# A fused attention and expert kernel: five expert units from a table built beside the scatters, and turned remainders by transposes

## The chip, the cores and the metric

The kernel runs on one core of a Trainium2 chip. The time is the device time of one execution in microseconds (us). Five engines of the core work side by side, each through its own instructions in order: PE (TensorE, the matrix engine), ACT (ScalarE), DVE (VectorE), POOL (GpSimd) and SP (SyncE, which issues most DMAs). PSUM is the memory that PE writes its results to, in banks of 2 KB a partition; SBUF is the memory that the engines compute from. An engine's instruction waits at the head of its queue until the semaphores it needs are up.

## The reference

An attention with a threshold, and behind it a mixture of experts in which each token goes to one expert:

```
q, k, v: [8, 8, 576, 64]; x: 4608 tokens of 512; 8 experts, w1 [8, 512, 1024], w2 [8, 1024, 512]
scores = q @ k.T / 8
scores = where(scores >= max(scores) - tau, scores, -1e9)
x = (softmax(scores) @ v), heads side by side         # tokens of 512
e = argmax(x @ w_gate);  gate = softmax(x @ w_gate)[e];  eom = sigmoid(x @ w_output_gate)
out[token] = gate * eom[e] * (relu(x @ w1[e]) @ w2[e])
```

## The kernel before

**Attention.** The first half of the program runs over 32 units, each one head of two batches (the two halves of the partitions). A period m takes two units in nine steps, s = 0 to 8: four tiles of 128 queries of the one, a tile with the last 64 queries of both, four tiles of the other. There are sixteen periods. In a step PE computes the scores of tile g (L137, into PSUM tiles `ps`), DVE copies them with the row maximum (L148), POOL makes the threshold (L155), ACT takes the exponentials (L162) and DVE masks and sums (L175). Two steps later the tile of probabilities `p` is turned, keys onto partitions: eight blocks of 64 columns by 16 transposes (L217, `pt`, copied out by ACT at L220 or L225), and the remainder, the last 128 columns, by `remainder`. In between PE issues matmuls of `av_units` (L239), a generator that multiplies the turned probabilities `PTa` (256 queries) or `PTb` (320 queries) with the values into one bank `pa`: ten matmuls to a half, of which a step takes 4, 6 or 8, so that a half stays open from one step to the next; the copy at L244 ends it.

The remainder comes in two forms. In a step that also issues the rows of x (s = 1 and 5; L330 copies them out of the banks `pr` and `pa`), two transposes of 128x64 are put in unused columns of these banks (L201) and ACT copies them from there (L202). In every other step two matmuls with the identity as the moving side (L206, 64x128, PE in another row and column mode than its neighbours) write `pr`, and ACT copies that (L209).

**Routing.** A `Router` holds a queue of generators that are advanced a step at a time between other work: they find each token's expert (`route`), place it by a running count (`place`, `init_units`, `finish`), and scatter its row to a DRAM buffer `xs` with POOL DMAs (L473). `finish` writes zero rows behind each expert's last token (the pads, again L473), then computes on DVE, in operations on 1x8 to 1x352 elements, which expert and which row each later unit has.

**Experts.** A unit is a run of rows of one expert. It has eight steps f; in a step `first(f)` does twelve matmuls (L945 to L947: three for each of four chunks, since each operand is split in a high and a low part), ACT makes `hh` by relu (L949) and DVE the rest `hl` (L950). `second` of the step before it does three matmuls of 512 columns for each tile of 128 rows (L966 to L968). Steps 5 and 6 turn the next unit's rows (`prep`, L931), and each weight chunk (four to a unit, 1 MB) is split by ACT (L761) and DVE (L764). The next unit's rows are gathered by one DMA that SP issues (L908). Units 0 and 1 are the first 384 rows of experts 0 and 1 (the early units, gathered from tokens that are already scattered); then six units of 512 with static experts, four `Pair` units of 256 rows whose expert is read from a table, and one `Flex` of 128 rows interleaved with unit 10: 4992 rows in all, 52 weight chunks, where there are 4608 tokens. `rest` is a loop for what is left over. The transition is the part from unit 0 to the start of unit 2: the last routing, the token scatters, the pads and the table happen there.

Of the kernel before, what the change touches and what calls it, by code (L numbers as in the profile page):

```python
# [8 lines left out]
F32 = mybir.dt.float32  # L9
# [11 lines left out]
class Attention:  # L21
# [12 lines left out]
    def __init__(self, ctx, tc, ident, qkv, tau, wg, shape, router):  # L34
# [45 lines left out]
        self.loaded, self.sums, self.rinv, self.lt, self.sumup = {}, {}, {}, {}, None  # L80
# [116 lines left out]
    def remainder(self, dst, p, pair=None):  # L197
# [12 lines left out]

    def blocks(self, dst, p, late=False):
        nc, id_, hs, RB = self.nc, self.ident, self.half, self.NK - 1
        pt = self.ps_t.tile([P, 1024], F32, name="pt")
        for b in range(RB):
            for h in range(2):
                o, k0 = h * 512 + b * 64, (b + b // 4) * P
                nc.tensor.transpose(pt[:, o : o + 64], p[hs[h], k0 : k0 + P], id_[hs[h], hs[h]])  # L217
        if len(dst) == 1:
# [8 lines left out]
    def av_units(self, u):  # L227
# [4 lines left out]
        for half in range(2):  # L232
            PT, q0 = (self.PTb, self.QA) if half else (self.PTa, 0)
            N = PT.shape[2]
            pa = self.ps_a.tile([P, 512], F32, name="pa")
            for i in range(self.NB + 1):
# [6 lines left out]
                if i == self.NB:  # L243
                    nc.scalar.copy(X[:, q0 : q0 + N], pa[:, 0:N])  # L244
                yield
# [57 lines left out]

    def run(self, hooks):
# [4 lines left out]
        for g in range(G + self.TAIL):  # L309
# [55 lines left out]
            if lu is not None and lu in xls:  # L365
                self.logits(lu, xls.pop(lu))
                if lu == self.nu - 1:
                    self.logit_sums(0)
                    self.logit_sums(1)
# [8 lines left out]
class Router:  # L378
    NPAIR = 4

    def __init__(self, ctx, tc, ntok, E, DM, early, esize, cut):
# [12 lines left out]
        self.A = E * self.CAP + 2 * P  # L394
# [9 lines left out]
        self.ecap = c.tile([P, E], F32, name="ecap")  # L404
        self.asc = c.tile([P, E], F32, name="asc")
# [3 lines left out]
        for e in range(E):  # L409
            nc.gpsimd.memset(self.ebase[:, e : e + 1], float(e * self.CAP + self.base[e]))  # L410
            nc.gpsimd.memset(self.elim[:, e : e + 1], float(e * self.CAP + esize) if e < early else -1.0)
# [19 lines left out]
        self.prows = c.tile([1, 2, self.NPAIR], I32, name="pairs")  # L431
        self.total = c.tile([1, 1], I32, name="total")
        self.odd = ctx.enter_context(tc.tile_pool(name="rodd", bufs=1))
        self.ripe = False
        self.xrows, self.queue, self.pending, self.placed, self.tables = {}, [], None, None, []
        self.gate, self.kind = None, None

# [11 lines left out]
    def init_units(self):  # L449
        E = self.E  # L450
        parts = [(self.xs[self.A :, :], "itok")]
        for e in range(self.early, E + 1):
            n = self.base[e] if e < E else 2 * P
            parts.append((self.xs[e * self.CAP : e * self.CAP + n, :], "itok"))
        for dst, group in parts:
            for r in range(0, dst.shape[0], P):
# [4 lines left out]
                yield None  # L461
# [23 lines left out]
    def route(self, bp, rows, LX):  # L485
# [77 lines left out]
        G.tensor_copy(rows[:, :, self.DM], sc)  # L563
        yield False
# [30 lines left out]
    def finish(self, ctx):  # L595
        nc, E = self.nc, self.E
        sm = ctx.enter_context(self.tc.tile_pool(name="rfin", bufs=1, reuse_waits="tile"))
        V = nc.vector
        pad = sm.tile([P, E], F32, name="padf")
        padi = sm.tile([P, E], I32, name="padi")  # L600
        V.tensor_scalar(pad, self.cnt, self.pid, None, op0=ALU.add)
        V.tensor_copy(padi, pad)
# [6 lines left out]
        row = lambda n, name, dt=F32: sm.tile([1, n], dt, name=name)  # L609
        ni, nj, nf, np, m0, v = row(E, "ni", I32), row(E, "nj", I32), row(E, "nf"), row(E, "np"), row(E, "m0"), row(E, "v")  # L610
        cp, ci, cm = row(E + 1, "cp"), row(E + 1, "ci"), row(E + 1, "cm")
        V.tensor_tensor(nf, self.cnt[0:1], self.ebase[0:1], op=ALU.subtract)
        V.tensor_scalar(nf, nf, float(P - 1), None, op0=ALU.add)
        V.tensor_copy(ni, nf)
        yield False
        V.tensor_scalar(ni, ni, 7, None, op0=ALU.arith_shift_right)
        V.tensor_scalar(ni, ni, 0, None, op0=ALU.max)
        V.tensor_scalar(nj, ni, 1, None, op0=ALU.arith_shift_right)
        V.tensor_copy(nf, ni)
        V.tensor_copy(np, nj)  # L620
        yield from self.sums(cp, np)
        yield from self.table(sm, "p", self.prows, cp, 2 * P, self.ebase[0:1])
        self.tables.append("p")
        yield False
        V.tensor_scalar(cm, cp, float(self.NPAIR), None, op0=ALU.min)
        V.tensor_tensor(m0, cm[:, 1:], cm[:, 0:E], op=ALU.subtract)
        V.scalar_tensor_tensor(nf, m0, -2.0, nf, op0=ALU.mult, op1=ALU.add)
        V.scalar_tensor_tensor(v, m0, float(2 * P), self.ebase[0:1], op0=ALU.mult, op1=ALU.add)
# [45 lines left out]
class Experts:  # L674
    RB, NW, YB = 4, 4, 4
    PAIRS = (2, 4, 6, 8)
    FLEX = 10
# [18 lines left out]
    def open(self):  # L696
# [7 lines left out]
        for name, bufs in (("y", 4), ("x", 2), ("h", 2)):  # L704
# [39 lines left out]
    def emit_out(self, y, keys, n):  # L744
        nc, DM = self.nc, self.rt.DM
        yo = self.yp.tile([P, DM], F32, name="yo")
        sc = keys[0][:, n : n + 1]
        if n % 2:
            nc.scalar.activation(yo, y, AF.Copy, scale=sc)
        else:  # L750
# [3 lines left out]
            out_offset=bass.IndirectOffsetOnAxis(ap=keys[1][:, n : n + 1], axis=0),  # L754
# [15 lines left out]
    def first_chunk(self):  # L770
        w, (a, b) = self.split_w(self.raws.pop(0))
        self.ready.append(w)
        self.done = 2
# [3 lines left out]
    def begin(self, nstatic):  # L777
        rt = self.rt
        make = [lambda e=e: Base(self, e) for e in range(rt.E)]
        for s, at in enumerate(self.PAIRS):  # L780
            make.insert(rt.early + at, lambda s=s: Pair(self, s))
        self.make, self.units, self.flex = make, {}, None
        self.seq = []
        for i in range(len(make)):
            for g in range(4):
                self.seq.append((i, g))
                if i == self.FLEX:
                    self.seq.append((None, g))
        self.nload = self.done = self.used = 0
        self.halves, self.ready = [], []  # L790
        for _ in range(self.RB):
            self.load_next()

    def unit(self, i):
        if i is None:
            if self.flex is None:
                self.flex = Flex(self, 0)
            return self.flex
# [4 lines left out]
    def load_next(self):  # L803
        if self.nload < len(self.seq):
            i, g = self.seq[self.nload]
            self.nload += 1
            self.raws.append(self.load(self.unit(i).e, g, self.rt.gate if self.nload <= self.RB else None))

    def split_until(self, n):
        while self.done < min(n, 2 * len(self.seq)):  # L810
# [6 lines left out]
            if not self.halves:  # L817
                self.load_next()
# [5 lines left out]
    def run(self):  # L824
        rt, nun = self.rt, len(self.make)
        self.split_until(4)
        prev, fin = None, False
        for i in range(nun):
            b, final = self.unit(i), i == nun - 1
            late = 4 if i == rt.early - 1 else 0  # L830
            for f in range(8):
# [3 lines left out]
                if i == self.FLEX + 1 and f == 1:  # L835
                    self.flex.second(turned)
                    self.flex.finish()
# [11 lines left out]
                if i == self.FLEX and f % 2:  # L849
                    self.flex.step(f // 2, self.take())  # L850
                if i == self.FLEX + 1 and f == 0:
                    turned = self.flex.transposed()
# [3 lines left out]
                self.split_until(2 * self.used + (4 if f % 2 else 3))  # L856
# [4 lines left out]
                if i == self.FLEX - 1 and f == 7:  # L861
                    self.flex.gather()
                if i == self.FLEX and f == 0:
                    self.flex.prep()
# [4 lines left out]
                for _ in range(4):  # L869
                    rt.advance(True)  # L870
                if not rt.queue and not fin:
# [294 lines left out]
```

## Time and profile before

| | before |
|---|---|
| time, median of 3 (lowest, highest) | 968.69 us (967.88, 969.49) |
| the profiled execution: time, span | 967.93 us, 966.2 us |
| PE busy | 948.4 us (98%) |
| DVE, ACT, POOL busy | 690.3 us (71%), 592.3 us (61%), 339.0 us (35%) |
| granted TensorE clock, mean | 0.995 |
| instructions | 22101 |

A row of a timeline gives the start, the duration, the engine, the line, the operation with its output and inputs by the program's names, its size and a count of equal instructions that follow each other; behind it in brackets the idle time of the engine ahead of it and what ended it. The duration of a matmul covers its way through the array, so that matmuls that follow each other overlap; their price is the distance of two starts. The 1.7 us between the span and the profiled time lie outside the trace.

### The profile page before, as it was taken

The page shows a single profiled execution, that of the slowest core. Times are in us where ns is not written, and L with a number is a line of the kernel's source. Part 1 is how long each engine was busy: PE and PEld are TensorE (multiplying, and loading weights), DVE is VectorE, ACT ScalarE, POOL GpSimd, SP SyncE. Part 2 cuts the span into 40 slices and gives each one's busy share as a digit, 9 for nine tenths or more (in the row PEclk, how much of TensorE's full clock was granted, in tenths as well). Part 3 has the DMA queues.
Part 4 walks back from the last instruction along what each step waited for, and adds up shares of the span by engine and source line. Part 5 has one row for each costly group of instructions (what it writes and reads, how often), then busy time and mean ns, then how long its engine had stood idle before and what let it go on. Part 6 is the DMA issues. An engine that isn't in the chain of part 4 may idle for free. (4 is left out here: it accounts for less than half of the span.)

```text
span 966.2 us, 22101 instructions
## 1 busy us (share of the span) xinstructions
PE 948.4 (98%) x8491; PEld 716.2 (74%) x8491; DVE 690.3 (71%) x1631; ACT 592.3 (61%) x1052; POOL 339.0 (35%) x573
## 2 busy tenths in 40 slices
PE   9999999999999999999989899999999999999996
PEld 5677676776766767667668787778878878878785
DVE  7999999999999999999865752535535535536721
ACT  6888888888879888788853342324424434435521
POOL 4343443656736675466635410202102002002001
PEclk9999999999999999999999999999999999999998
DMA  4355443133331342317157753426526526537401
GB/s 161 102 165 159 147 151 90 57 93 110 122 93 54 115 132 79 93 54 271 60 188 227 252 180 112 150 90 219 192 84 222 167 89 237 166 98 231 152 11 44
DMA packets 87531, 130.88 MB, mean 135 GB/s; under 512 B 24831, under 2 KB 51711, under 8 KB 87424
## 3 DMA queue, kind: packets, MB, share of 16 engines
q1 hardware_dynamic: 62096, 103.70, 34.1%
q0 software_dynamic: 6640, 21.02, 5.7%
q10 hardware_dynamic: 18688, 4.72, 2.0%
q8 instruction: 68, 1.11, 0.5%
q14 instruction: 39, 0.32, 0.1%
HBM read 95.26 MB, written 30.22 MB: 130 GB/s over the span
## 5 line engine op out<-in xcount | busy, mean ns | idle before, releaser
L162 ACT ACTIVATE p<-s,mn 128x576 f32<-128x576 f32 x288 | 207.7, 791 | 43.2 <-DVE s L148 42.4
L148 DVE TENSOR_SCALAR_CACHE_REDUCE s<-ps 128x576 f32<-128x576 f32 x288 | 205.9, 750 | 26.9 <-PE ps L137 26.3
L175 DVE SCALAR_TENSOR_TENSOR p<-s,thr,p 128x576 f32<-128x576 f32 x288 | 223.5, 812 | 0.0
L137 PE MATMUL ps<-qk 64*128 64x288 f32 (+1 forms) x1280 | 181.7, 419 | 0.1
L949 ACT ACTIVATE hh<-ph 128x512 fp32r<-128x512 f32 (+2 forms) x95 | 48.6, 511 | 208.3 <-PE ph L947 204.1
L155 POOL TENSOR_SCALAR thr<-mn,tau_sb 128x2 f32<-128x2 f32 x144 | 107.1, 744 | 194.9 <-DVE s L148 192.5
L752 POOL DMA_INDIRECT out_dram<-yo,kid x39 | 43.0, 1104 | 367.6 <-DVE yo L751 272.3
L950 DVE SCALAR_TENSOR_TENSOR hl<-ph,hh 128x512 fp32r<-128x512 f32 (+2 forms) x95 | 54.9, 578 | 141.2 <-ACT hh L949 141.1
L945 PE MATMUL ph<-xh,w1h 128*128 128x512 f32 (+2 forms) x380 | 134.7, 354 | 0.6 <-ACT xl L330 0.6
L946 PE MATMUL ph<-xl,w1h 128*128 128x512 f32 (+2 forms) x380 | 132.0, 347 | 0.2 <-DVE xl L764 0.2
L947 PE MATMUL ph<-xh,w1l 128*128 128x512 f32 (+2 forms) x380 | 131.9, 347 | 0.0
L966 PE MATMUL py<-w2h,hh 128*128 128x512 f32 x301 | 119.9, 398 | 3.2 <-ACT hh L949 3.2
L968 PE MATMUL py<-w2h,hl 128*128 128x512 f32 x301 | 119.8, 398 | 3.1 <-DVE hl L950 3.1
L137 PEld LDWEIGHTS ps<-qk 64*128 64x128 f32 (+1 forms) x1280 | 107.5, 177 | 18.4 <-DVE s L148 3.7
L967 PE MATMUL py<-w2l,hh 128*128 128x512 f32 x301 | 119.2, 396 | 0.0
L217 PE MATMUL pt<-ident,p 64*128 64x64 f32 x2304 | 100.9, 227 | 0.0
L239 PE MATMUL pa<-PTb,vld 128*64 128x320 f32 x640 | 100.0, 442 | 0.2 <-DMA PTb<-PTc 0.2
L217 PEld LDWEIGHTS pt<-ident,p 64*128 64x128 f32 x2304 | 82.8, 139 | 19.5 <-issue 13.2
L764 DVE TENSOR_TENSOR w1l<-r,w1h 128x1024 fp32r<-128x1024 f32 x52 | 63.6, 1223 | 23.3 <-ACT w1h L761 22.4
L945 PEld LDWEIGHTS ph<-xh,w1h 128*128 128x128 f32 x380 | 71.3, 188 | 11.9 <-ACT xl L330 0.8
L239 PE MATMUL pa<-PTa,vld 128*64 128x256 f32 x640 | 79.7, 387 | 0.2 <-ACT PTb L202 0.2
L946 PEld LDWEIGHTS ph<-xl,w1h 128*128 128x128 f32 x380 | 71.4, 188 | 10.1 <-DVE xl L764 0.6
(221 smaller groups left out, 1502.3 us busy)
## 6 DMA issues: line engine op xcount, KB each, us to landing
r<-in_moe_w_dram SPq DMA_DIRECT2D x104, 512.0 KB, 3.9
qk<-in_qkv_dram SPq DMA_DIRECT2D x31, 608.0 KB, 4.6
vld<-in_qkv_dram SPq DMA_DIRECT2D x32, 320.0 KB, 4.4
xs<-zrow SPq DMA_DIRECT2D x32, 257.0 KB, 2.7
xg<-xs SPq DMA_DIRECT2D x6, 1028.0 KB
PTb<-PTc ACTq DMA_DIRECT2D x16, 288.0 KB, 4.7
xg<-xs SPq DMA_DIRECT2D x4, 514.0 KB, 4.3
xg<-xs SPq DMA_DIRECT2D x2, 771.0 KB
```

The costliest lines, as they stand in the source:

```text
L137: nc.tensor.matmul(ps[a][rows, o : o + HS], q[pp, t * P : t * P + w], k[pp, k0 : k0 + HS], start=True, stop=True)
L148: nc.vector.tensor_scalar(s, ps[a][:, c0 : c0 + S], SC, None, op0=ALU.mult, op1=ALU.min, accum_out=mn[:, a : a + 1])
L162: self.nc.scalar.activation(e, s, AF.Exp, bias=mn[:, a : a + 1], scale=-1.0)
L175: nc.vector.scalar_tensor_tensor(e, s, thr[:, a : a + 1], e, op0=ALU.is_le, op1=ALU.mult, accum_out=acc[:, a : a + 1])
L217: nc.tensor.transpose(pt[:, o : o + 64], p[hs[h], k0 : k0 + P], id_[hs[h], hs[h]])
L239: nc.tensor.matmul(pa[self.half[a], 0:N], vm[:, kb, a], PT[:, 4 * a + kb if i else self.NK - 1], start=(i == 0), stop=(i == self.NB), skip ...
L945: nc.tensor.matmul(ph, w1h[:, c, fs], self.xh[:, c, 0:N], start=(c == 0), stop=False)
L946: nc.tensor.matmul(ph, w1h[:, c, fs], self.xl[:, c, 0:N], start=False, stop=False)
L947: nc.tensor.matmul(ph, w1l[:, c, fs], self.xh[:, c, 0:N], start=False, stop=(c == 3))
L966: nc.tensor.matmul(Y, hh[:, ts], wh, start=(f == 0), stop=False)
L967: nc.tensor.matmul(Y, hh[:, ts], wl, start=False, stop=False)
L968: nc.tensor.matmul(Y, hl[:, ts], wh, start=False, stop=(f == 7))
```

## The change

*Remainder.* In the steps s = 3, 6 and 8 a half of the values' product stays open, that is, `pa` is in use and will be added to in the next step. There the two 64x128 matmuls are replaced by the two 128x64 transposes of the other form; the first goes to columns 320 to 383 of the open bank `pa`, the second to `pr`, and ACT copies each out with a copy of 128x64. There are 47 such steps.

*Units.* The early units have 256 rows rather than 384. All later units take expert and row from a table that `choose` writes on DVE (eleven small operations to a slot), a slot at a time, advanced beside the scatters, from the last routing on. Slots have 448, 512, 384 or 256 rows; the order of the units is 448, 512, 256, 448, 256, 512, 256, 448, 384, 256, 512, which makes 4800 rows with the early units, 52 weight chunks again, and no Flex ahead of the loop. The gather of unit 2 waits for the token scatters and not for the pads. A slot of 448 is `Turned`: its second matmuls keep the weights and move the rows (twelve of 448 columns), four copies bring the result to SBUF, and sixteen transposes of 128x128 (`flip`, steps 1 and 2 of the next unit) turn it back ahead of the output. A weight load is issued only when the unit's slot is known.

```
-        rt = Router(ctx, tc, out.shape[0], w1.shape[0], out.shape[1], 2, 3 * P, nbp - 2)
+        rt = Router(ctx, tc, out.shape[0], w1.shape[0], out.shape[1], 2, 2 * P, nbp - 2)
@@ Attention.remainder, av_units, run
         if pair:
             for h in range(2):
-                nc.tensor.transpose(pair[h], p[hs[h], M : M + P], self.ident[hs[h], hs[h]])
-            return lambda h: nc.scalar.copy(dst[0][:, RB, 64 * h : 64 * h + 64], pair[h])
+                nc.tensor.matmul(
+                    pair[h], p[hs[h], M : M + P], self.ident[hs[h], hs[h]], start=h == 1 or fresh, stop=True,
+                    is_transpose=True, skip_group_check=True,
+                )
+            at = lambda h: dst[0][:, RB, 64 * h : 64 * h + 64] if len(dst) == 1 else dst[h][:, RB]
+            return lambda h: nc.scalar.copy(at(h), pair[h])
...
-                self.remainder(dst, p)
-                self.blocks(dst, p, u2 % 2 and t2 == 2)
+                if s in self.AV and self.pa is not None:
+                    o = self.S - self.QA
+                    rest = self.ps_r.tile([P, 512], F32, name="pr")
+                    out = self.remainder(dst, p, [self.pa[:, o : o + 64], rest[:, 0:64]], fresh=False)
+                    self.blocks(dst, p, u2 % 2 and t2 == 2, out)
+                else:
+                    self.remainder(dst, p)
+                    self.blocks(dst, p, u2 % 2 and t2 == 2)
@@ Router.choose, one slot of z rows
+            V.scalar_tensor_tensor(key, st[:, 1], float(z), st[:, 0], op0=ALU.is_ge, op1=ALU.mult)
+            V.tensor_reduce(mx, key, axis=AX.X, op=ALU.max)
+            V.scalar_tensor_tensor(cand, key, mx, self.desc[0:1], op0=ALU.is_equal, op1=ALU.mult)
...
+            self.tables.append(k)
@@ Experts
-    PAIRS = (2, 4, 6, 8)
-    FLEX = 10
+    UNITS = (0, 3, 7, 1, 8, 4, 9, 2, 6, 10, 5)
...
-                for _ in range(4):
+                for _ in range(6 if rt.last else 3 if i or f else 0):
                     rt.advance(True)
+                rt.aside(1 if rt.tables and i < rt.early else 2 if i else 4)
+                self.load_next()
@@ Pair.load, Turned.second, Turned.flip
+        rt.after(ins, [x for _, x in rt.tok])
+        if self.s == 0:
+            rt.tc.declare_no_dep(ins.ins, group="pad", reason="rows of their own")
+        else:
+            rt.after(ins, rt.pads)
...
+        for c, Y in enumerate(self.Y):
+            wh, wl = (w[:, f % 2, c * P : c * P + P] for w in (w2h, w2l))
+            nc.tensor.matmul(Y[:, 0:N], wh, hh[:, 0:N], start=(f == 0), stop=False)
+            nc.tensor.matmul(Y[:, 0:N], wh, hl[:, 0:N], start=False, stop=False)
+            nc.tensor.matmul(Y[:, 0:N], wl, hh[:, 0:N], start=False, stop=(f == 7))
...
+            for c in range(4):
+                nc.tensor.transpose(pt[:, c * P : c * P + P], self.yt[:, c, o : o + P], ex.ident)
+            ex.emit_out(pt, self.keys, t, slice(0, P if t else 64))
```

On PE, in steps 6 and 7 of a period, the rows read before as follows (remainder at L206, blocks at L217, scores of the next step at L137, values at L239):

```order
L206 MATMUL pr<-ident,p 64x128 [waits DVE_49,Activation_49]
L206 MATMUL pr<-ident,p 64x128 [waits DVE_49]
L217 MATMUL pt<-ident,p 128x64 [waits Activation_49]
L217 MATMUL pt<-ident,p 128x64 x15
L137 MATMUL ps<-qk 128x288 [waits DVE_49] x2
L137 MATMUL ps<-qk 128x288 x2
L239 MATMUL pa<-PTa,vld 64x256 x6
```

The same place on PE in the changed kernel, where the lines are L201, L221, L137 and L246:

```order
L201 MATMUL pa<-ident,p 128x64 [waits DVE_49]
L201 MATMUL pr<-ident,p 128x64 [waits Activation_49]
L221 MATMUL pt<-ident,p 128x64 [waits Activation_49]
L221 MATMUL pt<-ident,p 128x64 x15
L137 MATMUL ps<-qk 128x288 [waits DVE_49] x2
L137 MATMUL ps<-qk 128x288 x2
L246 MATMUL pa<-PTa,vld 64x256 [waits Activation_49]
L246 MATMUL pa<-PTa,vld 64x256 x5
```

The first product with the values in step 7 has got a wait on ACT; the value that it waits for is the one that ACT's copy of the remainder out of `pa` raises. Steps 4 and 0 (of the next period), behind steps 3 and 8, read alike.

On DVE, in the transition, the table stood before in long pieces between two low parts of weight chunks (L764), behind the pads (L639 to L667):

```order
L764 TENSOR_TENSOR w1l<-r_8454,w1h 128x1024
L639 TENSOR_TENSOR ci<-ci,nf 1x1 x2
L631 CAST total<-ci 1x1
L654 TENSOR_TENSOR inas<-sid,ci 1x352
L655 TENSOR_TENSOR inbs<-sid,ci 1x352
L656 TENSOR_TENSOR inas<-inas,inbs 1x352
```

In the changed kernel the operations of `choose` (L643 to L655) lie in pieces of four to seven between the rest of the hidden rows (`hl`, L992) and the low parts (L819), from the step behind the last routing on:

```order
L992 SCALAR_TENSOR_TENSOR hl<-ph,hh 128x256
L819 TENSOR_TENSOR w2l<-r_8485,w2h 128x1024
L653 TENSOR_SCALAR picks<-got 1x1
L654 CAST picks<-got 1x1
L655 SCALAR_TENSOR_TENSOR st<-cand,st 1x24
L992 SCALAR_TENSOR_TENSOR hl<-ph,hh 128x256
L819 TENSOR_TENSOR w1l<-r_8648,w1h 128x1024
L643 SCALAR_TENSOR_TENSOR key<-st 1x8
L644 TENSOR_REDUCE mx<-key 1x1
L645 SCALAR_TENSOR_TENSOR cand<-key,mx,desc 1x8
L646 TENSOR_REDUCE cm<-cand 1x1
```

What moved is the table, from behind the pads to beside the scatters, and from a few blocks with 1x352 operations to many blocks of 1x8.

## Rows read from the trace of the kernel before

**Rows 1.** Windows view: per stretch, its length, busy time of each engine, granted clock.

```profile
100.00:200.00 100.00, 99.96 (x1276) 69.56 (x1273) 94.85 (x268) 84.19 (x161) 47.51 (x81) 1.00 0.37 112
500.00:530.00 30.00, 27.85 (x151) 23.91 (x150) 17.97 (x37) 12.09 (x20) 15.22 (x24) 0.94 0.71 221
```

**Rows 2.** Timeline of PE, steps 3 and 4 of a period.

```profile
102.48 0.39 PE L206 MATMUL pr<-ident,p 128*64 128x128 f32 x4
102.80 0.71 PE L217 MATMUL pt<-ident,p 64*128 64x64 f32 x16
...
104.57 0.49 PE L239 MATMUL pa<-PTb,vld 128*64 128x320 f32 x2
```

**Rows 3.** Timeline of PE, steps 5 to 7 of the same period.

```profile
109.20 0.22 PE L201 MATMUL pa<-ident,p 64*128 64x64 f32 x1
109.25 0.66 PE L217 MATMUL pt<-ident,p 64*128 64x64 f32 x16
...
113.89 1.52 PE L239 MATMUL pa<-PTa,vld 128*64 128x256 f32 x12
```

**Rows 4.** Timeline of ACT, the copies of the remainder in steps 3 and 6.

```profile
103.61 0.25 ACT L209 COPY PTa<-pr 128x128 f32<-128x128 f32 x1
...
114.08 0.23 ACT L209 COPY PTb<-pr 128x64 f32<-128x64 f32 x1
```

**Rows 5.** Timelines of ACT and PE in the transition: a relu, and the matmul behind it.

```profile
502.88 0.47 ACT L949 ACTIVATE hh<-ph 128x384 fp32r<-128x384 f32 x1
...
503.40 0.79 PE L966 MATMUL py<-w2h,hh 128*128 128x512 f32 x1 [2.15 <-ACT hh L949]
```

**Rows 6.** Timeline of PE, first matmuls of units 0 (its step 1), 2, 3, 4, 5.

```profile
494.71 0.44 PE L945 MATMUL ph<-xh,w1h 128*128 128x384 f32 x1 [0.64 <-ACT xl L330]
...
568.63 0.50 PE L945 MATMUL ph<-xh,w1h 128*128 128x512 f32 x1
...
614.91 0.40 PE L945 MATMUL ph<-xh,w1h 128*128 128x512 f32 x1
...
660.86 0.28 PE L945 MATMUL ph<-xh,w1h 128*128 128x256 f32 x1
...
686.42 0.40 PE L945 MATMUL ph<-xh,w1h 128*128 128x512 f32 x1
```

**Rows 7.** Timeline of PE, unit 10 with the Flex, and unit 11 to the end.

```profile
871.14 0.28 PE L945 MATMUL ph<-xh,w1h 128*128 128x256 f32 x1
...
872.43 0.28 PE L947 MATMUL ph<-xh,w1l 128*128 128x256 f32 x1
...
906.45 0.38 PE L1053 MATMUL px<-ident,hr 128*128 128x128 f32 x2
...
906.78 0.28 PE L1039 MATMUL ph<-w1h,xfl 128*128 128x256 f32 x1
...
909.49 0.40 PE L945 MATMUL ph<-xh,w1h 128*128 128x512 f32 x1
...
952.79 0.39 PE L966 MATMUL py<-w2h,hh 128*128 128x512 f32 x1
...
958.16 0.40 PE L968 MATMUL py<-w2h,hl 128*128 128x512 f32 x1
```

**Rows 8.** Timeline of POOL: last token scatter, last pad, unit 2's rows taken up.

```profile
522.82 0.99 POOL L473 DMA_INDIRECT xs<-rows,dsti  x1 [0.16 <-issue]
...
538.55 0.97 POOL L473 DMA_INDIRECT xs<-zrow,padi  x1 [0.30 <-issue]
...
550.15 0.19 POOL L740 COPY ksc<-xg 128x4 f32<-128x4 f32 x1 [6.43 <-DMA xg<-xs]
```

**Rows 9.** Groups by line on DVE from 490 to 575 us: count, busy, mean ns, idle.

```profile
L764 DVE TENSOR_TENSOR w2l<-r,w2h 128x1024 fp32r<-128x1024 f32 x10 | 12.2, 1221 | 2.1 <-ACT w2h L761 1.9
...
L950 DVE SCALAR_TENSOR_TENSOR hl<-ph,hh 128x384 fp32r<-128x384 f32 x15 | 8.3, 552 | 11.9 <-ACT hh L949 11.8
...
L639 DVE TENSOR_TENSOR cp<-cp,np 1x1 f32<-1x1 f32 x8 | 1.2, 147 | 0.2
```

More of the change, by code (lines that the diff above doesn't have):

```diff
@@ L217, in blocks @@
                 nc.tensor.transpose(pt[:, o : o + 64], p[hs[h], k0 : k0 + P], id_[hs[h], hs[h]])
+        for h in range(2) if out else ():
+            out(h)
         if len(dst) == 1:
@@ L302, in logit_sums, with last_sums @@
             rt.queue.append(rt.route(bp, rt.xrows[bp], LX))
+    def last_sums(self):
+        yield True
+        for k in range(2):
+            self.logit_sums(k)
+            yield True
     def run(self, hooks):
@@ L451, in init_units @@
         parts = [(self.xs[self.A :, :], "itok")]
-        for e in range(self.early, E + 1):
-            n = self.base[e] if e < E else 2 * P
-            parts.append((self.xs[e * self.CAP : e * self.CAP + n, :], "itok"))
+        for e in range(E + 1):
+            r0 = e * self.CAP + (self.base[e] if e < self.early else 0)
+            parts.append((self.xs[r0 : r0 + self.SAFE, :], "itok"))
         for dst, group in parts:
@@ L563, in route @@
         G.tensor_copy(rows[:, :, self.DM], sc)
+        if bp == self.cut + 1:
+            self.side.append(self.choose())
+            self.last = True
         yield False
@@ L608, in finish @@
                 yield False
[L609 to L613, printed above, removed]
+        while not self.chosen:
+            yield False
+        ni, nf, v, ci, st = row(E, "ni", I32), row(E, "nf"), row(E, "v"), row(E + 1, "ci"), self.st
+        V.tensor_scalar(nf, st[:, 0], float(P - 1), 0.0, op0=ALU.add, op1=ALU.max)
         V.tensor_copy(ni, nf)
-        yield False
         V.tensor_scalar(ni, ni, 7, None, op0=ALU.arith_shift_right)
-        V.tensor_scalar(ni, ni, 0, None, op0=ALU.max)
-        V.tensor_scalar(nj, ni, 1, None, op0=ALU.arith_shift_right)
         V.tensor_copy(nf, ni)
[L620 to L628, printed above, removed]
+        V.tensor_scalar(v, st[:, 2], -1.0, dummy, op0=ALU.mult, op1=ALU.add)
         yield False
@@ L772, in first_chunk, with begin @@
         self.ready.append(w)
-        self.done = 2
+        self.done, self.nsplit = 2, 1
         self.load_next()
         return a + b
-    def begin(self, nstatic):
+    def begin(self):
         rt = self.rt
[L779 to L789, printed above, removed]
+        make = [lambda e=e: Base(self, e) for e in range(rt.early)]
+        make += [lambda s=s: (Turned if rt.SLOTS[s] % P else Pair)(self, s) for s in self.UNITS]
+        self.known = lambda i: i < rt.early or self.UNITS[i - rt.early] in rt.tables
+        self.make, self.units = make, {}
+        self.seq = [(i, g) for i in range(len(make)) for g in range(4)]
+        self.nload = self.done = self.used = self.nsplit = 0
         self.halves, self.ready = [], []
-        for _ in range(self.RB):
-            self.load_next()
+        self.load_next()
     def unit(self, i):
[L795 to L798, printed above, removed]
         if i not in self.units:
@@ L993, in __init__ @@
     def __init__(self, ex, s):
[L994 to L1005 removed]
+        self.ex, self.nc, self.s = ex, ex.nc, s
@@ L1115, in build @@
             ex.run()
-        ex.rest(1)
+        ex.rest()
 def lay_out(q, k, v, wg, wog):
```

178 lines of the change are left out of this document (132 added, 46 removed).

## The prediction

> **What bounds the kernel now.** I read the windows first. In the attention PE is busy 99.96 us of 100 at a granted clock of 1.00, while DVE has 94.85, ACT 84.19 [rows 1]: PE sets the end there, with DVE 5% and ACT 16% behind it. So what PE saves in a step counts in full only while no other engine's result comes later; and a new wait of PE costs in full. In the transition PE has 27.85 of 30 us, and the mean clock of 0.94 says that 3.6 us of it ran at half clock (0.06 x 30 / 0.5), which lost some 1.8 us more [rows 1]. Then I read the timelines of PE for prices. A 512-column matmul starts every (958.16 - 952.79) / 23 = 0.2335 us, a 256-column one every (872.43 - 871.14) / 11 = 0.117 [rows 7], about 0.456 ns a column; 384 columns then take 0.174 and 448 take 0.204, both estimates from these two. A unit of 512 rows takes 192 x 0.2335 = 44.8 us, so a row costs 0.0875 us. What the next unit's rows add: from unit 3 to unit 4 45.95 us less 44.8, so 1.1 for 256 rows; from unit 4 to unit 5 25.56 us [rows 6], of which 96 x 0.117 + 48 x 0.2335 + 1.40 (the 512 unit's second step 7 that falls into it is 1.40 longer than its own) = 23.8 to be taken off, so 1.7 for 512 rows. By columns I take 1.4 for 384 and 1.6 for 448.
>
> **Attention.** 47 steps change (15 of s = 6 with a wait to look at, one in the first period without, 15 of s = 3, 16 of s = 8). *Saved:* from the first L206 to the first L217 PE takes 0.32 us [rows 2]; two transposes take 0.05, where they lie in parallel row groups [rows 3]. The upper bound is 0.27 a step. The new pair lies between the same neighbours in the other direction: it follows L239, another mode than its own, so that the change of mode which the old pair paid on leaving is now paid on entering, and a part of the 0.27 stays. I take 0.2, with 0.16 and 0.27 as ends: 47 x 0.2 = 9.4.
>
> *Added:* the product with the values of the next step waits for ACT's copy out of `pa`, which waits in its queue behind that step's exponentials. In s = 6 this copy ran from 114.08 to 114.31 [rows 4], and PE began the product at 113.89 [rows 3]. A relu that ended at 503.35 let PE begin at 503.40 [rows 5], so 0.05 for the notice: PE can begin at 114.36, 0.47 later than before. Since ACT's chain up to there starts from a PE result (the rows of x in s = 5), what PE saves between them is lost with it. Behind the waiting matmul stand the rest of the products, the next remainder and the next scores, for which DVE and ACT wait: it costs in full, 15 x 0.47 = 7.0, and it also swallows the saving of s = 6 itself. In s = 3 the copy starts at 103.61 and the product at 104.57 [rows 2, 4]: 0.25 for the copy leaves 0.7, less the 0.2 saved. No wait there; s = 8 has as much. Sum: 15 x 0.47 - 15 x 0.2 (s = 3) - 16 x 0.2 (s = 8) - 0.2 (s = 6 of the first period) = +0.7. If ACT comes earlier by half a microsecond (its copies are two of 128x64 where there was one of 128x128, so no earlier by itself) nothing waits and the sum is -9.4; if it comes later by 0.3, +5.
>
> A rule of the Trainium skill speaks against this change: the page "PSUM — Partial Sum Buffer", section "PSUM bank collisions raise a hardware error", says that two engines may not touch one bank in the same quadrant of partitions at once, even in other columns, and asks for a semaphore by bank and quadrant. By it the wait is due behind each of the 47 copies, though the columns differ, and the sum is the +0.7 above; without it the sum would be the -9.4. The order of instructions shows that wait; no run has timed it yet. The Trainium skill's page "TensorEngine Tiling (Array Packing)", section "Key Properties", says that a mode switch needs a drain: a switch kept means the lower saving, 7.5 rather than 12.7 us over 47 steps, and the sum +1.9; a switch gone means -1.6.
>
> **Transition.** Units 0 and 1 have 256 rows for 384. From step 1 of unit 0 to unit 2 it took 568.63 - 494.71 = 73.92 us [rows 6]. A step of 384 rows takes 12 x 0.174 + 9 x 0.2335 = 4.19, fifteen of them 62.8, with 1.4 and 1.7 for the two preparations 65.9: 8.0 us were waits and half clock, the largest of them the 2.15 in which PE waited for a relu that had waited for the routing [rows 5]. After: a step of 256 rows takes 12 x 0.117 + 6 x 0.2335 = 2.81, fifteen 42.2, with 1.1 and 1.6 44.9. Of the waits the 2.15 and the half clock stay (4.0); those that the long table operations made go. DVE is the new question: ten and nine low parts at 1.22, fifteen `hl` at 0.55 or less [rows 9], some 80 operations of `choose` at 0.15 to 0.19, the rest of routing and outputs come to about 45 us for 50 us of PE. I put 1 us for that, 5.0 in all; the lower bound is 2, the upper 14 (rival 2). Before it, unit 0's step 0 has 12 matmuls of 256 columns for 384, -0.7. Gain: 73.9 + 0.7 - 49.9 = 24.7.
>
> Unit 2 would then start at about 544. Its rows must be there 8 us earlier, for its preparation. Before they came at 550.15, 11.6 us behind the last pad's start, and the last token scatter started at 522.82 [rows 8]. Without the pads in the chain the same 11.6 us would put them at 534.4. So the gather hides, but by 1 to 2 us only.
>
> **From unit 2 on.** 4288 rows for 4224: +64 x 0.0875 = +5.6. The Flex of 128 rows took 38.35 us (871.14 to 909.49) less 23.8 less 1.7 = 12.8, and unit 11 to its end 48.9 less 44.8 less 1.4 = 2.7 [rows 7]: 15.5, of which its rows are 11.2, so -4.3 over the rows. Unit 1's last second step is shorter by three matmuls, -0.7. Three turned units add 48 transposes; two of them and a 256-column matmul took 0.33 (906.45 to 906.78) [rows 7], so 0.107 each, +5.1. Ten preparations for nine, by the above, +1.1. Sum +6.8. The turned units' matmuls themselves cost by the row as others do; their four copies and outputs lie on ACT and DVE, which have half their time free there. Eight more zeroing DMAs of the start and the slot reads on SP lie beside the attention and the units.
>
> **Sum.** -24.7 + 6.8 + 0.7 = -17.2. The profiled execution took 967.93 us, 0.76 below the median: 950.7 beside it, 951.5 as a median.
>
> **Rivals.** (1) *The copies out of the open bank come early enough:* for it, ACT has 16% free [rows 1]; against it, s = 6 misses by 0.47. Then attention gives 9.4 rather than taking 0.7: 941.4. (2) *The transition keeps its stalls:* scatters, table, SP's slot reads and unit 2's gather form a chain that the shorter units outrun, and a long wait of PE brings the half clock behind it, as at 503. If unit 2's rows come 9 us late, waits are 14 us: 960.5. For it, the gather hides by only 1 to 2 us and DVE is nearly full; against it, 11.6 us behind the pads contained the table, which now comes earlier. (3) *Slower than before:* the waits on ACT in steps 4, 7 and 0 feed back, since PE's later scores make the exponentials later, ACT's copy is queued behind these, and all three steps wait. To eat the 17.9 us that the experts give, 47 waits would have to cost 17.9 / 47 + 0.2 = 0.58 us each, so ACT would have to fall behind in every step by 1 us against [rows 2, 4]; its 16% free speak against it. At 0.6 us each: 970. (4) *The slots don't cover the counts* of some expert, and the loop at the end turns: at least one Flex (15.5 us) and its weight loads, which nothing would cover and which may take up to the 23.8 us in which a unit of 256 rows gets its four chunks today: 967 to 991, in the middle 979. 4800 rows for 4608 tokens over eight experts leave 192, so it needs counts that fit badly.
>
> **How the numbers follow.** Forecast 951.5, its own range 946 to 957: 55%. Rival 1 14%, rival 2 21%, rival 3 7%, rival 4 3%. The range of 941 to 962 leaves out the far ends. Of a change within 0.2%, about what a measurement of this kernel can tell from none, I give 2%; faster 0.91, slower 0.07 (rivals 3 in most of its cases, and 4).
>
> **What would show it.** Right: no idle time of PE in s = 4 and 0; in s = 7 a wait of PE of about half a microsecond released by ACT's copy out of `pa`, and a period's length unchanged within 0.2 us; unit 2 starting at 543 to 546 us; from there to the end 404 to 405 us; no turn of the loop. Wrong: periods shorter by 0.6 us (rival 1), a wait of PE of several microseconds in unit 1 put down to a DMA or DVE, or a granted clock below 1 behind it (rival 2), waits on ACT in all three steps (rival 3), output rows written after the last unit (rival 4). The weakest numbers are the 0.47, a difference of two starts in one period, and the 5.0 us of waits that I leave in the transition.

## The result, and the profile after

The changed kernel takes 956.32 us (median of 4, 955.07 to 957.61), the kernel before 968.76 beside it (967.88 to 969.49): a ratio of 0.9872, 95% interval 0.9855 to 0.9889. The profiled execution took 955.07 us, its span is 953.0. Forecast were 951.5 us and a faster kernel; the gain is 12.4 us where 17.2 were forecast. The profile tells the three stages apart.

**Attention.** The timeline of PE, steps 3 and 4 of the period of [rows 2]:

```profile
102.55 0.27 PE L201 MATMUL pa<-ident,p 64*128 64x64 f32 x1
102.56 0.27 PE L201 MATMUL pr<-ident,p 64*128 64x64 f32 x1
102.66 0.66 PE L221 MATMUL pt<-ident,p 64*128 64x64 f32 x16
103.25 1.20 PE L137 MATMUL ps<-qk 64*64 64x288 f32 x16
104.39 1.03 PE L246 MATMUL pa<-PTb,vld 128*64 128x320 f32 x6
```

The same view, steps 6 and 7, and the timeline of ACT beside it (to be read against [rows 3, 4]):

```profile
110.81 1.08 PE L246 MATMUL pa<-PTa,vld 128*64 128x256 f32 x8
111.83 0.27 PE L201 MATMUL pa<-ident,p 64*128 64x64 f32 x1
...
112.43 1.28 PE L137 MATMUL ps<-qk 64*128 64x288 f32 x8
114.19 1.52 PE L246 MATMUL pa<-PTa,vld 128*64 128x256 f32 x12 [0.47 <-ACT PTb L206]
```

```profile
111.23 2.81 ACT L162 ACTIVATE p<-s,mn 128x576 f32<-128x576 f32 x4
113.91 0.23 ACT L206 COPY PTb<-pa 128x64 f32<-128x64 f32 x1
```

From its first score matmul to that of the next step, each of the steps 3, 6 and 8 is 0.155 us shorter (step 3: 3.05 for 3.21). In step 7 PE stands for 0.47 us until ACT's copy out of `pa`, queued behind four exponentials, ends at 114.14, and begins at 114.19. Step 7 takes 3.96 us for 3.33, steps 6 and 7 together 6.82 for 6.34. A quiet period, one without routing in it, takes 29.77 us for 29.60, and periods 2 to 15 together 420.7 for 419.1: the attention got 1.6 us longer. (Period 1 varies by more than 1 us from execution to execution of any of these kernels and is left out of such sums.)

**Transition.** The timeline of PE, from step 1 of unit 0 to unit 2:

```profile
494.55 0.39 PE L987 MATMUL ph<-xh,w1h 128*128 128x256 f32 x1
...
498.64 0.38 PE L989 MATMUL ph<-xh,w1l 128*128 128x256 f32 x1 [0.80 <-DVE w1l L819]
...
537.68 0.39 PE L1010 MATMUL py<-w2h,hl 128*128 128x512 f32 x1
541.47 0.90 PE L1081 MATMUL px<-ident,xg 64*128 64x64 f32 x12 [3.41 <-DMA xg<-xs]
...
543.64 0.36 PE L1081 MATMUL px<-ident,xg 64*128 64x64 f32 x1 [0.75 <-issue]
...
544.32 0.41 PE L988 MATMUL ph<-xl,w1h 128*128 128x256 f32 x1
544.53 0.41 PE L989 MATMUL ph<-xh,w1l 128*128 128x256 f32 x1
...
549.02 0.47 PE L987 MATMUL ph<-xh,w1h 128*128 128x448 f32 x1
```

It took 54.5 us for 73.9 [rows 6]; forecast were 49.9. PE stood some 4.3 us for unit 2's rows (for the last 0.75 of them the profile names no releaser), and behind that the 256-column matmuls start 0.21 apart, not 0.117 [rows 7]: half clock. The steps 6 and 7 of unit 1 are 6.7 us longer than their matmuls and transposes. The wait for the relu at 503 [rows 5], which I had kept, is gone; in the same step, step 2 of unit 0, PE now waits 0.80 us for a low part on DVE, and in step 2 of unit 1 it waits 0.71 us for `hl`. These two steps are 1.1 and 1.0 us longer than their matmuls.

The timelines of SP and POOL, to be read against [rows 8], and the windows (PE to POOL busy, granted clock, DMA share, GB/s) of the same stretch:

```profile
499.75 31.69 SPq L773 DMA_DIRECT2D r<-in_moe_w_dram  x13
535.85 1.82 SPq L1051 DMA_DIRECT2D xg<-xs  x3
```

```profile
514.50 1.09 POOL L501 DMA_INDIRECT xs<-rows,dsti  x1 [2.49 <-DVE mx L644]
...
527.86 1.85 POOL L501 DMA_INDIRECT xs<-rows,dsti  x1 [0.31 <-DMA xs<-rows,dsti]
```

```profile
510.00:515.00 5.00, 5.00 (x45) 4.32 (x45) 3.49 (x16) 3.08 (x7) 2.20 (x9) 1.00 0.37 105
515.00:520.00 5.00, 4.72 (x29) 3.80 (x28) 4.79 (x16) 2.21 (x4) 4.09 (x4) 1.00 0.51 141
520.00:525.00 5.00, 4.91 (x33) 4.15 (x32) 4.69 (x14) 4.31 (x7) 4.09 (x4) 1.00 1.02 339
525.00:530.00 5.00, 4.38 (x27) 3.92 (x28) 4.79 (x18) 2.13 (x3) 4.10 (x3) 1.00 1.05 349
530.00:535.00 5.00, 5.00 (x34) 4.51 (x33) 3.87 (x11) 2.42 (x4) 4.07 (x4) 1.00 1.06 385
535.00:540.00 5.00, 3.06 (x20) 2.42 (x18) 2.25 (x6) 0.62 (x2) 3.97 (x4) 1.00 1.03 332
540.00:545.00 5.00, 2.62 (x19) 2.17 (x20) 0.00 (x0) 0.00 (x0) 3.24 (x5) 0.55 0.99 369
```

The last token scatter is issued at 527.86, 5.0 us later than before (the first one 3.2 us later, 514.50 for 511.33, and from the first to the last it took 13.4 us for 11.5), the gather 8.0 us behind it, and its last piece is taken up at 543.6. The DMA engines are half idle to 520 us and full from there to 545. Unit 2's weights can't be asked for before its expert is picked: of the thirteen loads (half a MB each) of the first row, SP issued five to 509, stood until it had read the pick at 517, and issued the other eight, all four chunks of unit 2, from 518 to 531.

**From unit 2 on** the kernel takes 953.0 - 549.02 = 404.0 us; forecast were 404.4 (397.6 before plus 6.8). There are 39 output scatters, as many as the thirteen units ahead of the loop have tiles: the loop doesn't turn.

### The profile page after: what moved, and what is told of

Read it like the earlier page. It is cut to its first block, busy times and chain, and to the rows that moved or that the text cites. A ratio compares the mean times of both kernels' runs of the same rounds, so it can differ in the third digit from the quotient of the medians.

```text
span 953.0 us, 22402 instructions
## 1 busy us (share of the span) xinstructions
PE 931.5 (98%) x8477; PEld 712.4 (75%) x8477; DVE 705.8 (74%) x1752; ACT 597.2 (63%) x1105; POOL 349.1 (37%) x581
## 5 line engine op out<-in xcount | busy, mean ns | idle before, releaser
L137 PE MATMUL ps<-qk 64*128 64x288 f32 (+1 forms) x1280 | 182.9, 419 | 0.5 <-DVE s L148 0.5
L991 ACT ACTIVATE hh<-ph 128x256 fp32r<-128x256 f32 (+3 forms) x103 | 49.8, 483 | 183.9 <-PE ph L989 181.1
L987 PE MATMUL ph<-xh,w1h 128*128 128x256 f32 (+3 forms) x412 | 140.3, 340 | 0.0
L989 PE MATMUL ph<-xh,w1l 128*128 128x256 f32 (+3 forms) x412 | 137.2, 333 | 0.8 <-DVE w1l L819 0.8
L988 PE MATMUL ph<-xl,w1h 128*128 128x256 f32 (+3 forms) x412 | 137.3, 333 | 0.2 <-DVE xl L819 0.2
L992 DVE SCALAR_TENSOR_TENSOR hl<-ph,hh 128x256 fp32r<-128x256 f32 (+3 forms) x103 | 55.6, 540 | 102.0 <-ACT hh L991 101.3
L137 PEld LDWEIGHTS ps<-qk 64*128 64x128 f32 (+1 forms) x1280 | 109.3, 177 | 18.3 <-DVE s L148 4.3
L246 PE MATMUL pa<-PTb,vld 128*64 128x320 f32 x640 | 100.0, 442 | 0.5 <-ACT PTa L206 0.5
L221 PE MATMUL pt<-ident,p 64*128 64x64 f32 x2304 | 99.0, 225 | 0.0
L221 PEld LDWEIGHTS pt<-ident,p 64*128 64x128 f32 x2304 | 83.4, 139 | 11.4 <-issue 9.4
L1010 PE MATMUL py<-w2h,hl 128*128 128x512 f32 x214 | 84.7, 396 | 1.0 <-DVE hl L992 1.0
L246 PE MATMUL pa<-PTa,vld 128*64 128x256 f32 x640 | 79.7, 387 | 6.0 <-ACT PTb L206 6.0
L1008 PE MATMUL py<-w2h,hh 128*128 128x512 f32 x214 | 84.8, 396 | 0.0
L987 PEld LDWEIGHTS ph<-xh,w1h 128*128 128x128 f32 x412 | 77.9, 189 | 9.0
L1009 PE MATMUL py<-w2l,hh 128*128 128x512 f32 x214 | 84.5, 395 | 0.0
L819 DVE TENSOR_TENSOR w1l<-r,w1h 128x1024 fp32r<-128x1024 f32 x52 | 64.4, 1238 | 26.4 <-ACT w1h L816 20.5
L988 PEld LDWEIGHTS ph<-xl,w1h 128*128 128x128 f32 x412 | 78.0, 189 | 7.7 <-DVE xl L819 0.6
```

The costliest lines, as they stand in the source:

```text
L137: nc.tensor.matmul(ps[a][rows, o : o + HS], q[pp, t * P : t * P + w], k[pp, k0 : k0 + HS], start=True, stop=True)
L246: nc.tensor.matmul(pa[self.half[a], 0:N], vm[:, kb, a], PT[:, 4 * a + kb if i else self.NK - 1], start=(i == 0), stop=(i == self.NB), skip ...
L987: nc.tensor.matmul(ph, w1h[:, c, fs], self.xh[:, c, 0:N], start=(c == 0), stop=False)
L988: nc.tensor.matmul(ph, w1h[:, c, fs], self.xl[:, c, 0:N], start=False, stop=False)
L989: nc.tensor.matmul(ph, w1l[:, c, fs], self.xh[:, c, 0:N], start=False, stop=(c == 3))
L1008: nc.tensor.matmul(Y, hh[:, ts], wh, start=(f == 0), stop=False)
```

## The experiments

Ratios are to runs of the kernel before on the same chip. "Periods" are 2 to 15 of the attention; "unit 2" is the start of its first matmul in the one profiled execution; "two chunks" means two of unit 2's weight chunks behind its rows.

| kernel | periods, us | unit 2, us | median, us | ratio (95%) |
|---|---|---|---|---|
| before (profiled for the forecast) | 419.1 | 568.6 | 968.76 | |
| before, second profile | 419.1 | 565.1 | 968.18 | 1.0005 |
| changed | 420.7 | 549.0 | 956.32 | 0.9872 (0.9855 to 0.9889) |
| old remainder everywhere | 419.2 | 548.2 | 955.50 | 0.9868 (0.9846 to 0.9890) |
| old remainder in step 6 | 416.5 | 547.9 | 950.81 | 0.9815 (0.9797 to 0.9834) |
| copies ahead in step 6 | 417.3 | 548.6 | 953.32 | 0.9839 (0.9820 to 0.9857) |
| sums at once | 420.6 | 550.2 | 955.72 | 0.9861 (0.9841 to 0.9880) |
| pads behind the rows | 420.6 | 548.8 | 954.74 | 0.9901 (0.9885 to 0.9916) |
| two chunks | 420.7 | 543.3 | 950.08 | 0.9854 (0.9840 to 0.9867) |
| two chunks, pads, old in step 6 | 416.1 | 537.8 | 944.28 | 0.9795 (0.9782 to 0.9809) |
| two chunks, pads, copies ahead | 415.9 | 538.5 | 944.54 | 0.9795 (0.9782 to 0.9809) |
| changed, again | 420.6 | 549.7 | 955.59 | 0.9921 (0.9903 to 0.9939) |
| two chunks, old everywhere | 419.2 | 541.4 | 948.82 | 0.9848 (0.9833 to 0.9864) |
| two chunks, old in step 6 | 416.1 | 539.9 | 945.84 | 0.9817 (0.9801 to 0.9834) |

The kernel before had a median of 968.7 us beside the runs from "old remainder everywhere" to "sums at once", and 964.2 beside those below them up to the last row; so times, not ratios, are compared across the two groups, and the changed kernel was run again in the second (955.59 against 956.32).

**The attention: which copy, and why it is late.** First the expert part alone.

```
-                if s in self.AV and self.pa is not None:
+                if False:
```

> The changed kernel with every remainder in its old form (two 64x128 matmuls), so only the expert part of the change is left. Theory: the attention part of the change costs 1.6 us net (47 savings of 0.155 us against fifteen waits), so the last scores start at 475.9 us as in the kernel before, not at 477.5, and the time is 954.7. Rival: the attention part is worth its savings and the 1.6 us come from elsewhere; then the time is above 956.3, up to 963.6.

955.50 us, periods as before the change to 0.1 us. The attention part costs 1.5 us there; in the time this is 0.8, less than the scatter of the runs, and unit 2 starts 0.8 earlier. The same with two chunks behind unit 2's rows (the edit is shown below):

> Two weight chunks behind unit 2's rows, and every remainder in its old form: the expert part alone, with the wait for unit 2's rows out of the way, so that the attention's length reaches the end. Theory: the attention part of the change costs 1.5 us (periods 2 to 15: 420.7 us with it, 419.2 without): 1.5 us less than with two chunks behind the rows and the transposes, a ratio of 0.984. Rival: the attention part saves its 47 transposes' worth on the whole and the time is above that, a ratio of 0.987 or more.

948.82 against 950.08 with the transposes: 1.3 us, as the theory has it.

```
-                if s in self.AV and self.pa is not None:
+                if s in self.AV and s != 6 and self.pa is not None:
```

> The changed kernel with the old form of the remainder in step 6 alone; steps 3 and 8 keep the transposes. Theory: the wait for ACT's copy out of the open bank exists in step 7 only. Steps 6 and 7 together go back from 6.82 us to 6.34 in each of 15 periods, 7.2 us less 0.2 for the first period's step 6: 949.3. Rival: ACT is late in general, the wait moves to the step behind 8, and nothing or little is gained: 954 to 956.

950.81. The wait in step 7 is gone (3.33 us), steps 3 and 8 keep their saving, a quiet period takes 29.30 us, and the wait moved nowhere. Periods: -4.1 us (one of them was 0.4 longer than its like). The sum of 7.2 less 0.2 took all periods for quiet ones: those gave 0.47 each, the seven with routing in them (29.5 to 31.0 us) only 0.02 to 0.33; there other steps grew instead (in one, step 8 to 3.28 us from 3.13 and the step 0 behind it to 3.89 from 3.68). The time gained 5.5, and the profiled execution, 954.54 us, is the slowest of five: in it unit 2 starts only 1.1 us earlier than in the changed kernel, since PE stands 4.7 and 1.7 us ahead of turning its rows.

```
-            if g < G:
+            mid = g < G and s == 6 and m > 0
+            if g < G and not mid:
                 pr[g] = self.exps(u, t, *st[g])
@@ blocks(), behind the two copies of the remainder: the exponentials of step 6, then the copy of the blocks
+        if mid:
+            mid()
```

> The changed kernel with all 47 steps kept, but in step 6 ACT's two remainder copies are put ahead of that step's exponentials rather than behind them. Theory: the copy is late only because of the exponentials queued ahead of it on ACT; without them it ends 1.4 us earlier, PE's wait in step 7 goes and the saving of step 6 stays: 2.86 + 3.33 us for steps 6 and 7, 15 x 0.63 = 9.5 us, 946.8. Rival: exponentials that come half a microsecond later delay DVE's masks and with them the next remainder; then half of it or less is left, 951 or more.

953.32. A timeline of ACT in this kernel, then of PE, step 6 and the start of step 7:

```profile
112.08 1.48 ACT L162 ACTIVATE p<-s,mn 128x576 f32<-128x576 f32 x2
113.42 0.24 ACT L206 COPY PTb<-pa 128x64 f32<-128x64 f32 x1
```

```profile
112.67 0.27 PE L201 MATMUL pa<-ident,p 64*128 64x64 f32 x1
...
114.49 1.51 PE L248 MATMUL pa<-PTa,vld 128*64 128x256 f32 x12
```

Two exponentials instead of four are ahead of the copy; it ends at 113.66, 0.8 us before PE asks for the bank, and PE doesn't stand. That shows the queue on ACT as the cause. A quiet period takes 29.23 us. Step 7 keeps 0.1 us over 3.33; it lies in the scores ahead of the product (1.21 us from start to start for 1.12), and I have no cause for it. As a whole kernel it gained 3.0 us where the expectation had 9.5: one period of its profiled execution was 1.8 us longer than the others, by a wait of 1.71 for an exponential, and the rest was lost to unit 2's rows.

**The transition: who makes unit 2's rows late.**

```
-                    rt.queue.append(self.last_sums())
+                    self.logit_sums(0)
+                    self.logit_sums(1)
```

> The changed kernel with the last sums of the logits issued at once, as before the change, not from the queue behind three low parts of weight chunks. Theory: routing, scatters and the gather of unit 2 form one chain, and its start on DVE sets when unit 2's rows come: scatters 3.2 us earlier, rows some 3 us earlier, PE's wait of 3.4 us for them nearly gone and with it the half clock behind it (1.7 us): unit 2 starts at 544 to 546 us instead of 549.0, time 952. Rival: the DMA engines, which are full from 535 to 545 us, set when the rows come: unit 2 starts at 548 to 549, time 956.

955.72. The scatters do start 2.2 us earlier (512.31), but the last is issued only 1.1 earlier (526.77), since two copies of unit 1's row keys on POOL (1.3 us) now lie between the second scatter and the third. The gather is issued 0.9 earlier, and still unit 2 starts at 550.2. My theory falls: an earlier start of the chain does not bring the rows earlier. That full DMA engines hold them back is not shown by this run; the one with two chunks, below, bears on it.

```
-                if not rt.queue and not fin:
+                if not rt.queue and not fin and (i, f) >= (1, 5):
```

> The changed kernel with the eight pads put behind the arrival of unit 2's rows on POOL. Since the last run refuted that DVE sets when these rows come, two theories are left. Full DMA engines: six of the eight pads (1.6 MB, 4.3 us at 370 GB/s) were under way ahead of the rows; without them the rows come 2 to 4 us earlier, unit 2 starts at 545 to 547 us, time 953. Chain of latencies: the gather is issued when the last token scatter has landed, which was issued ahead of the pads anyway; the rows come at most 1 us earlier, time 955 to 956.

954.74. The gather is issued at 535.67 (535.85 in the changed kernel), the last piece of the rows lands at 543.62 (and is taken up at 543.64 there). This execution came to step 1 of unit 0 0.9 us later than the other, so what is behind the last token scatter counts for 1 us or so, not for the 2 to 4 of the first theory. What is ahead of it:

```
-        while self.nload < min(len(self.seq), self.nsplit + self.RB):
+        while self.nload < min(len(self.seq), self.nsplit + (2 if self.nload >= 8 and not self.gone else self.RB)):
...
                     self.unit(i + 1).gather()
+                    self.gone = self.gone or i == 1
```

> The changed kernel with two of unit 2's four weight chunks (2 MB) issued behind the gather of its rows, where all four were issued between 517 and 531 us, beside the scatters. Full DMA engines: 2 MB are 5.7 us at 370 GB/s; scatters follow each other at 1.28 us again, the gather is issued at 531 to 532, the rows are there at about 537, PE's wait of 3.4 us and the half clock behind it go: unit 2 starts at 544 us, time 951. Chain of latencies: the rows come as late as now, unit 2 at 549, time 956.

950.08. SP's timeline, the windows from 525 us on, and PE's timeline in this kernel:

```profile
532.22 1.81 SPq L1052 DMA_DIRECT2D xg<-xs  x3
534.29 12.88 SPq L773 DMA_DIRECT2D r<-in_moe_w_dram  x8
```

```profile
525.00:530.00 5.00, 4.71 (x30) 4.25 (x31) 4.79 (x14) 1.78 (x3) 4.15 (x3) 1.00 0.89 341
530.00:535.00 5.00, 5.00 (x34) 4.48 (x33) 3.61 (x12) 2.64 (x4) 4.09 (x4) 1.00 0.57 128
535.00:540.00 5.00, 4.07 (x34) 3.18 (x33) 2.46 (x7) 1.18 (x4) 3.78 (x5) 1.00 1.07 346
540.00:545.00 5.00, 4.97 (x39) 3.90 (x37) 3.78 (x12) 3.33 (x9) 3.16 (x5) 1.00 1.06 364
```

```profile
537.70 0.58 PE L1082 MATMUL px<-ident,xg 64*128 64x64 f32 x12
538.72 0.27 PE L1082 MATMUL px<-ident,xg 64*128 64x64 f32 x1 [0.44 <-DMA xg<-xs]
539.49 0.27 PE L1082 MATMUL px<-ident,xg 64*128 64x64 f32 x1 [0.49 <-DMA xg<-xs]
```

The DMA share falls to 0.57 ahead of the gather, which is issued 3.6 us earlier; PE waits 0.9 us in all, the clock stays at 1.00, and unit 2 starts at 543.3 where the forecast of the changed kernel had 544. The scatters did not come closer, though: the last one is issued at 527.52, against 527.86. It is their landing that was late. The DMA view of the last token scatter (its last number is the median us from issue to landing, here of one), first in the second run of the changed kernel, "changed, again", where it is issued at 528.16, then with two chunks:

```profile
xs<-rows,dsti POOLq DMA_INDIRECT x1, 7.2
```

```profile
xs<-rows,dsti POOLq DMA_INDIRECT x1, 4.3
```

In both the gather follows that landing by 0.4 us. Why some scatters keep POOL for longer than others is another matter, and the DMA engines are not the cause. Timelines of DVE and POOL in the changed kernel:

```profile
523.07 1.22 DVE L819 TENSOR_TENSOR w1l<-r,w1h 128x1024 fp32r<-128x1024 f32 x1
525.50 1.20 DVE L819 TENSOR_TENSOR w2l<-r,w2h 128x1024 fp32r<-128x1024 f32 x1
```

```profile
524.30 0.97 POOL L501 DMA_INDIRECT xs<-rows,dsti  x1 [0.30 <-issue]
525.58 1.98 POOL L501 DMA_INDIRECT xs<-rows,dsti  x1 [0.30 <-issue]
```

The DMA share was 1.09 during the short scatter and 1.08 during the long one. The long one began inside a low part of a weight chunk on DVE, and ended 0.85 us behind its end. Five of the nine token scatters in the changed kernel began so, two of nine in the kernel before: hence the 1.9 us that they took longer.

**Together.**

> Both of the above (two chunks and the pads behind unit 2's rows) and the old remainder in step 6. Theory: the attention's gain of 4.1 us (periods 2 to 15: 416.5 instead of 420.7 us) now reaches the end, since the rows of unit 2 no longer wait for full DMA engines: unit 2 starts at 539.5, time 946. Rival: the rows still set unit 2's start: 949 to 951.

944.28, unit 2 at 537.8.

> Two chunks and the pads behind unit 2's rows, and in step 6 ACT's two copies ahead of the exponentials, all 47 transposes kept. Theory: a period takes 29.23 us (29.30 with the old remainder in step 6, 29.77 with the change as it is), so 1 us less than the kernel with the old remainder in step 6: 945. Rival: the same or more, since the copy out of the open bank still costs 0.1 us in step 7: 946 to 948.

944.54, the same within the runs, so the 1 us of the theory is not there: with the old form in step 6, and with the copy moved, the attention takes as long (416.1 and 415.9). Both are 11 us faster than the changed kernel beside them.

> Two chunks behind unit 2's rows and the old remainder in step 6, the pads where the change puts them. Theory: the pads don't matter, since they are issued behind the last token scatter: ratio 0.980 as with the pads moved as well, unit 2 at 539. Rival: once the weight chunks are out of the way the pads are what fills the DMA engines: unit 2 1 to 2 us later, ratio 0.981 to 0.982.

945.84. 1.6 us more than with the pads moved as well. Of the difference between the two profiled executions (2.3 us) 1.0 lies in the first period. In both the gather is issued 37.8 us behind step 1 of unit 0; its last piece lands 7.7 us later here and 6.2 with the pads moved, which speaks for the rival. But it is 6.5 in "two chunks, old everywhere", where the pads are not moved, and 6.9 in "two chunks, pads, copies ahead", where they are. So whether the pads cost anything stays open.

> The changed kernel as it is, beside the two variants below on the same chip. Expected as measured: ratio to the kernel before 0.987, unit 2 at 549 us, PE's wait of 3 to 4 us for its rows and the half clock behind it.

955.59, unit 2 at 549.7, a wait of 5.03 us for its rows in one piece.

**The kernel before has two lengths.**

> The kernel before, profiled again: its times stand at 968.7 us beside some runs and at 964.3 beside others, while the changed kernel takes 955.6 to 956.3 beside both. If it takes 964 here, its trace shows where the 4.5 us lie. Theory: in the transition, the part from 494 to 569 us, where PE waits for single results and runs at half clock for a stretch; then unit 2 starts at 564 us instead of 568.6 and the rest is as long as before. Rival: in the attention's first period, which is up to 1 us longer or shorter from run to run, or spread over all of it.

This execution took 964.2 us; of the 8 two were at 963 to 964, the others at 966.7 to 969. Its timeline of PE, first matmul of unit 2:

```profile
565.09 0.50 PE L945 MATMUL ph<-xh,w1h 128*128 128x512 f32 x1
```

From step 1 of unit 0 it took 70.0 us, where it took 73.9 in the profile of the forecast: steps 3 and 4 of unit 1 lasted 4.18 each and not 5.60 and 6.78. The theory holds. So 3.9 us of the transition's 8.0 us of waits were not in every execution of the kernel before, and a gain of 12.4 us beside one group of runs is 8.7 beside the other (of the second group's own executions of the kernel before there is no trace). It isn't the chip: 968.7 and 964.2 both came as medians on one chip, and both lengths here on another. What starts these waits stays open; ACT's relu there came 5.8 us behind its last work.

## Why the prediction held, and where it was off

**Unit 2 to the end** was right in sum, 404.0 for 404.4: rows, flips, preparations and the Flex that went.

**Attention, mechanism right.** The wait is in step 7 alone and costs 0.48 us in steps 6 and 7 together, where 0.47 was forecast; steps 4 and 0 have none. The mis-sized term is the saving: 0.2 was taken, 0.155 measured. With 0.155 the sum comes to +2.1 instead of +0.7; measured are +1.6 in periods 2 to 15, since the seven with routing changed by -0.1 to +0.2 us where the quiet ones got 0.17 longer. From the start of the values' product to the next blocks in step 3 it is 1.34 us for 1.45 before, since the transposes begin 0.1 us later behind the product's start than L206 did (1.23 for 1.13). This is the lower end that the Trainium skill's rule on the drain at a mode switch ("TensorEngine Tiling (Array Packing)", "Key Properties") pointed to, with the switch moved from behind the pair to ahead of it; that the 0.1 us is the switch, no run shows by itself. The rule on banks and quadrants ("PSUM — Partial Sum Buffer", "PSUM bank collisions raise a hardware error", in the Trainium skill) agrees with the wait: PE stood for a copy of columns 320 to 383 before it wrote columns 0 to 255. The wait is one that the program holds; no run leaves it out.

**Transition, the step that failed.** "Without the pads in the chain the same 11.6 us would put them at 534.4. So the gather hides, but by 1 to 2 us only." The last scatter wasn't where it had been but 5.0 us later, and from it to the rows it took 13.6 us to the first and 15.8 to the last piece, not 11.6. I had taken both from a kernel whose unit 2 had a static expert, so that the weight loads were spread (twelve of half a MB over 41 us, from 495.55 on). In the changed kernel unit 2's come in a bunch once the pick is known, and the two chunks moved showed that 5.7 us of unit 2's start hang on this: not through the scatters' issue, but through their landing (7.2 us for 4.3). The case I had as rival 2 came about by half: 9.6 us of waits and half clock, where I had put 5.0 as likeliest and 14 for the rival. Of the 9.6, 6.7 are steps 6 and 7 of unit 1 and 2.1 the two steps that wait for DVE, for which I had taken 1. An error the other way stood against it: the wait for the relu and its half clock (4.0), which I kept, went, and 1.1 came in its place. By the forecast's own adding, the time without these 2.9 us would be about 959, above the 957 at which its range ended; that the range held was in part luck. (Some of the 2.9 us the wait for the rows would have taken up.) Nor do the runs bear out that the long table operations made the other 4.0 us of the old waits: the second profile of the kernel before has the same table and lacks 3.9 of them.

**Rivals 1, 3 and 4.** Rival 1 (no wait) is what "copies ahead" makes true. Rival 3 did not come: step 7 alone waits. The slots covered the counts.

## What to carry to other kernels

When a load's address becomes data, its time moves too: ask not only what the gather waits for but which other loads the same pick holds back, and what they collide with when all are let go at once. A spare corner of a bank in use isn't free: its next writer waits for the reader's whole queue, so look at what stands ahead of the copy, and move the copy or leave that one step out. A profile is one execution; where it holds waits of several us in a stage near a limit, a second one of the same kernel tells which of them are always there.

## What the runs showed of the hardware

The DMA engines at a share of 1.0 moved 332 to 385 GB/s in these stretches, and a token scatter among the bunched weight loads landed 7.2 us behind its issue, against 4.3 with half of these loads moved behind the rows.

How long an indirect DMA keeps POOL followed what DVE did, not how full the DMA engines were. In the fourteen traces, from 508 us on, there are 784 of them. The 336 that began inside a low part of a weight chunk on DVE (128x1024, 1.2 us), with 0.15 us or more of it left, ended 0.84 to 0.96 us behind that part's end; one of them took 1.89 us at a DMA share of 0.03 (511.33 in the kernel before). The others took 0.9 to 1.1 us, but for one of 2.06 that began 7 ns ahead of such a part.

PE stood from 538.1 to 541.5 us in the changed kernel, and the granted clock, 1.00 up to 540, was 0.55 from 540 to 545 us; with the wait cut to 0.9 us in two pieces it stayed at 1.00.
